# Thresholded attention and a maxout FFN on one core: another written order, other PSUM slots and other masks

## The chip, the core and the metric

The kernel runs on one core of one Trainium2 chip. The metric is the device time of one execution in microseconds (us). The core's engines run side by side, each through its own queue in program order, and wait for one another on semaphores: PE (TensorE, matrix products into PSUM; PEld is its loading of weights), DVE (VectorE), ACT (ScalarE), POOL (GpSimd) and SP (SyncE, which here only starts DMA transfers).

## The reference

```python
q, k, v: (8 batches, 8 heads, 576, 64), f32;   tau = 0.02
scores = matmul(q, k^T) / 8
keep   = scores >= max(scores, axis=-1) - tau        # else -1e9
attn   = exp(scores - max);  attn /= (sum(attn) + 1e-9)
x      = matmul(attn, v)                             # as 4608 tokens x 512
h      = maximum(maximum(x @ w1, x @ w2), x @ w3)    # 512 -> 768
out    = h @ w_out                                   # 768 -> 512
```

## The kernel before

The eight heads of a batch are taken as two quads of four heads, so there are 16 quads. Of each quad, q and k are loaded in f32, transposed on PE, copied out of PSUM, and multiplied. A *chunk* is 128 rows of queries for two of the heads; a quad has nine chunks (one of them holds the last 64 rows of all four heads), and each chunk has two *scores* of 128x576, so there are 144 chunks and 288 scores. A chunk's result P (bf16, normalized) goes through a DMA transpose from SBUF to SBUF, and with the transposed P of all nine chunks of a quad the product with v can be made (two products for each quad). The four products of a batch are the FFN's input x. The FFN of a batch is 18 hidden pieces (6 column blocks times w1, w2, w3) and two to four output pieces. The last batch's FFN is split in two parts (`SPLIT`), so that its first rows can start before the last chunks are through.

PSUM is used as four slots of 128x1024 f32. Every piece of PE work names the slot that it writes, and cannot start before the slot's former content has been read out.

The order of all this is not computed. It is a string, `ORDER`, that is read from left to right: each letter issues one step, on the engine that the step belongs to, and `_Ordered` chains the instructions of every engine in that order. Nearly all instructions pass through its helper, which is why the profile puts them all on L93. The order is thus binding within each engine (and within SP's queue of DMA starts), and free between engines. The letters, with the digit of the PSUM slot behind those of PE:

- PE: `S` one score (4 matmuls, 8 for a chunk of ninths), `T` a transposition of q or k, `O` a product with v, `F` the first half of an FFN piece and `B` its second half, `N` the out piece of a batch's last rows.
- DVE: `m` the pass over the score that gives the row maximum (z<-sc), `s` the small step from the maximum to the threshold (th), `k` the masked numerator (SCALAR_TENSOR_TENSOR with a sum), `r` the reciprocal, `c` k's way out of PSUM, `v` two thirds of the maxout, `w` a product's way out, `f` the last rows' way out.
- ACT: `e` the first pass over z, `n` the exponential with a sum, `a` q's way out of PSUM, `h` a third of the maxout, `x` a product's way out, `u` and `j` the FFN's output.
- POOL: `p` one of a chunk's two normalizing passes (P), `q` the swap of q's halves (qs; two early ones are on DVE), `y` and `z` casts of v and of the weights.
- SP: `l` loads of q, k and v, `g` loads of weights, `t` a chunk's transpose by DMA, `o` and `i` stores.

For each score one digit of `MASKED` chooses among four ways, which give the same numbers:

- 0: `m`, `s` on DVE; then two passes on ACT, `e` (a Prelu over z in SBUF, after which only the kept values count) and `n` (exponential with sum).
- 1 (masked): `m` on DVE; `e` on ACT is the exponential itself; `k` on DVE masks and sums. One pass less on ACT, one more on DVE.
- 2 and 3 (direct): as 0 and 1, but `e` reads the score from PSUM and not z, and 2 needs no `s`.

```python
def masked(g, idx, r):
    return by_mask[2 * number[g, idx] + r] in "13"
def direct(c, r):
    return by_mask[2 * number[c["g"], c["idx"]] + r] in "23"
...
def exponents(c, r):
    z = c["z", r]
    src, sign = (c[r], -1.0) if direct(c, r) else (z, 1.0)
```

So the PSUM slot of a score is free again after `m` (ways 0 and 1) or only after `e` (ways 2 and 3).

Buffers: z has 9 buffers, and 2 more in the weights' staging from the 73rd score on; P has 6; the quad's loads have 2 each; the transposed P has 2.

Of the kernel before, what the change touches and what calls it, by code (L numbers as in the profile page):

```python
# [21 lines left out]
FLAT = 2.0 ** -100  # L22

MASKED = """
232222322322222222021032222202332122123122200200111000000000100000000011
000010111020011000101000000001100001001000010011111100000000100100000000
110010030111000100010000000001010100001110001011010100110000000000000000
100101101011000000120000001010000000110011100000001110001000010011111021
"""


# [6 lines left out]
SPLIT = {7: ((0, 1), (2, 3, 4))}  # L38

ORDER = """  # L40
llllllglllT0laclT1laclzllqqS0qqS1meS2mS3lmlT0enlkS1ylmlT2eamelrnpS3leqlmnyS1qcapS0emtnrcS3pmnT2qmepgrelS1qya
gS0pmelT2mqnS3tcpemqS2nlkT1eytaS0rmnT1kpermS3yS2enczrmS1qT0enmepnqtS3nprmaymgpeS0lptS2mppT0mtpS1enencnqsS3re
rmtpS0mS1penmS3lqnsS2mtperpekzllmT0tmpenkT1pgS3eearnS0petmnqrS2meqlnpS3lmnplsS2cetpremS1pS0nmplermtzeS3mnS2p
mtnpmS3rkpS1leektS0emnrpmemptS1eekS2pO3mktS0rennmpermT2pnS1wptemS3prkyO0tmeakS2pgS1enxlnrmS0lpesS2mezT3mS1np
mgntspcS2eqrseT3mtpeS0srmapS1mnT2ptS3mnqO0ceqmeO1prswnptnkS3pxS0meF1meS2zBresmT0qghF3klpF2nkBtaS1sveS0pemF3B
nyrrsmyBepT1svS0hpcT2nS3zmaS1erpgsF2mntpsBmnS3yvF1etssT0myeBprS2cnpS3mnS0ympelF2epF3lmBnzslssvS0htBrqmeS2vpn
S1gF0sepmF3teqBmF2erssvpBtnBkphF0eS1vtS3znmF2nrBmqteS1rpvBnS3pmlnF0pmgeS1qsBsrhmS3pevS2npS1mF0npsO3ermpesmO2
zewepgsskBxtT3nF1vS2nklBarS0mlphS3mtepF2sS1rmnyBmetF3pvT0eBpcnS2tzT1nvS0asmzS3temS2qeS1meF0trkpmS3lenpBmnlys
reklpF1umerpskS3upBeoketmS0uS2umpS3tesmS1qeT0myO2nqlrsnlprcO3etqsmepwS0xptS1mnF3psnmS2BlerskpS1thF0meF3pmeBF
2ktnBveBsrS1nvpS0hmyF3emF2npBrssT0eprtvBaF1kS3nqvBeF0myhyS2kyleF3mBelBvnpS2snsS0vptemS1pnF3rmpT2tnBmpeF0scS1  # L50
htBrnmpF3erT2rpvlBasS1pstvnS2pmeF0pS3emtBqnmT2S1hcqS3empF2eS0rsqmtS1epsmBeF3pmnF0stsvBeBknF2klhF1BvelS0nrvpB
emT3pS2arvS0ptnS3mpnO1smtesrkpeF2swnlrpmeT0S1qtescS3epBmnpmnT0trskS3paS1umS0ulqmeS3lmyS1nopS2smelS0rmeS3psmn
O1ypersmqO2etkpemO0lewqxlknpS3tS1keF2momS3lexF0ktT1enkBercpnsBpumN1ertkphkF3jS0rursS1empBnmF2ptS0vpS1smeF3yt
BsnsmBpnvS0pT1hmF2atT3srepS0cF1eprBsmeqF3vnByBynvplS2nsS0plmhS1mteS2mF0nF3mteS1rrspBnmS2pelvBlepF1smT0leqBvl
aS2rkhF3oqnsS0mtS1epmBeqsF2ssmtS0epvBeyF1mnF3vpBesrS0ktphBermS1npT2svO0nytmpncT3eS1wF2nrmS0aBrsmnqF3vnT1pS0c
eBptsF2mhpS1eS3pmteS0qmBeO1spmnkteF3rvnpT0BsskapS2xvS0erS1qmtnS3pmnF2mqlespmeS1rtkBepresmT3puS1cuS0ptmnS3pS2
meyS1lrekpF0tnsmempO3lekteskO2nrsmpeBkpxrnwS1uptS3muS2pnmF0yoeS1mF3lesymBtnS2srkpS1hmBeF0spveF2ertBmpT3nrsvS
1paBlmpnS0tS3qhmF1epsmS2leBymF3tevF0nBknlS1rsvpS2esmqnBF3srmhpS1epS0tmeF2pssBrempBtesvS0ynF1mT3lnpBvF0lhsrcS
2tnT1mBnF3valS2nrBsqmeF0pvS1epS2meBptsmS3eqF1hmT2peBcS3tnskT2O0arkplnmO2lerpvewptS3xkpS1nF2meF0sstreBsmpS3nv
pBnmS1tS2hmT3eF0rmpnF1cBpnBrevptT3S2apvS0qmtS3S1enmqF2esrsqmiepmleS0soykeS1plBnmemtS3ukS0uT1snrlO2cpekynO1me  # L60
ymeF3pwxskteS0keS1BrrnkopmF2pmS0BqeuurtsmF1phS3srnpS2meT0ptBmeS3ykpaN2esvempF0tS1jkpF3ermBeS2ptvnS1pmBnS0rls
hsmpS2elF3mqntS1mpF0nsrBskpeF2lsmBetBpveF1yhvS3lnkS2lesF0mytnBmBerqsS3veF2lpvnF1pBsmT0htBceF3rT2vnpBsaS0pvnF
1qmtS2nBsrnmT0pS3hrcpF2esS1mpteS0rmpS3emBpntF1svqnS0ssBmpeoT2vO3lamtneF1wS0nrlBpmeS3qsrS2hsmS0pnmF1eptS3smeB
pmF2ntS0veS3rsmnpS1BnpO0veytrempS2empS3xsmS1tekF0nsknlT2rmpBelmlpnscS3quS1umyS2eorT0kpeO3tmeyO1ewlepsmF3etka
rknS2qklT0nBmxespcS2eryF0mpF1uskpuBtnS2BhmqF3nsvS0peS2srmtpF1eBmpeF0srvnBptS2hyS3pmeF1lmeBlBevtF3nkT2S0arrvp
BnS2mphS1smpF0ntS3smnpBmeF1lsT2esvlF3nrBrcptBnvpS2eS0qmlhS1tsnprsmT3F2epmS0aptBemF3yevS1oS0nqmBnpsrS2mnF1ptv
S0epmBeS3mthS2skeF0F1snmlBeklO3ersvpnrmByepF0swT2eqtBvnqF3ssrcS1hpiBmpT0S2vaptS1snmS0pnT3mqF2tecT1BarmS3pnS1
vqeS0mF2pesrmnptmS3npT1seS0qctBeymqermpS1eS3mpuF0nmtuskS1eS2klnS3smBesrsepO1upmemO2txrkpukeO3wnkpS0xS2emF3et
rmS1pnBssspmF2hS0rtepS3mnBpmF1etS0veF3mnN2rnpBpjF0evtF2esBkBkhF1nsvS3eBmBevO3hrkS2pwnS1mnF3prmS2eptsF0mnBpsS
1sevyS2terBmpeF3svS1iyepBmoS0yhmtF2ekF3nBsmS1ersBvpnF0pmeF2BvteS1hBmF3rsS0vpeF1rknpBBmnO2vhptO0xrpnS3pwS2trm  # L70
npS0mnF3pmteF1pBeBvtS0rS2vpS3empF1ktkF0kBereskpemBkperumO2uptO3xpN1wtenkO2jrF3pxF1hpF2nvF3tvF1rhF2pvF3pvF1hF
2tvF3vF1hF2voF3vF1ohF2vF3vF1hF2vO3vO1wF2xuuF1oF0hiF3vF1vF0hF3vF1vF0hF3vF1vF0hF3vF1vF0hF3vF1vF0huF3vF1ovF3uoF
0uoN1fjdi
"""


# [753 lines left out]
```

## Time and profile before

| | us |
|---|---|
| median of three runs | 446.71 |
| lowest and highest of them | 445.96 and 448.13 |
| span of the profiled execution, first to last instruction | 444.8 |
| PE busy in that span | 422.4 |
| ACT busy | 403.0 |
| DVE busy | 392.8 |
| POOL busy | 311.9 |

The profile gives no device time of its own for the profiled execution beside the span; the median of the runs lies 1.9 us above the span, for what stands around it and for the spread of the runs.

The page shows for every engine the busy tenths in 40 equal slices, the chain of work that ended last, groups of like instructions with the mean duration of one, and the DMA starts. A group's row has busy time, mean ns of one, and the idle time before its instructions with what ended it. Instructions on ACT and DVE overlap their neighbours a little, so what one instruction adds is the distance from its start to the next start, which is read from the timeline. The ends of matmuls are modelled, so that PE can look busy while it waits for a short time.

### The profile page before, as it was taken

The numbers are of one execution on the slowest core, as the hardware profiler recorded it, in microseconds if no ns is written. First come the engines' busy times: TensorE is split into PE (matmuls) and PEld (weight loads), VectorE is DVE, ScalarE is ACT, GpSimd is POOL, SyncE is SP. The second block draws the span as 40 slices with busy tenths as digits, with TensorE's granted clock in tenths as the row PEclk, the third lists the DMA queues.
The fourth block names the chain that finished last, engine by engine and source line by source line (L and its number), as shares of the span: only waits on it lengthen the run. The fifth ranks groups of instructions, "written<-read, shape, count | busy, mean of one in ns | idle before, by whom it ended". The sixth has DMA issues, their size and how long they took to land.

```text
span 444.8 us, 14254 instructions
## 1 busy us (share of the span) xinstructions
PE 422.4 (95%) x5188; PEld 320.2 (72%) x5190; DVE 392.8 (88%) x1228; ACT 403.0 (91%) x836; POOL 311.9 (70%) x420
## 2 busy tenths in 40 slices
PE   7767789999999999999999999999999999999996
PEld 6334347787788767787788777788688886787873
DVE  3887999999999999999999999998999998899642
ACT  3999999999999999999999999899999999987632
POOL 2799989997878687696785877676676685457400
PEclk8998999999999999999999999999999999999999
DMA  7999999999999999699899999989999977487633
GB/s 188 275 293 199 291 169 269 235 243 262 229 180 194 212 222 292 125 256 167 143 234 189 230 198 203 209 168 210 208 206 194 244 151 105 83 179 136 145 116 108
DMA packets 213959, 88.50 MB, mean 199 GB/s; under 512 B 189184, under 2 KB 202240, under 8 KB 213888
## 3 DMA queue, kind: packets, MB, share of 16 engines
q1 hardware_dynamic: 213360, 86.96, 95.9%
q8 instruction: 41, 0.67, 0.6%
q10 hardware_dynamic: 528, 0.62, 0.5%
q14 instruction: 30, 0.25, 0.2%
HBM read 35.65 MB, written 9.44 MB: 101 GB/s over the span
## 4 chain that ended last, share of the span: by engine, by line
PE 86%; ACT 5%; DVE 4%; issue 2%; DMA 1%; SPq 0%; DVEq 0%; ACTq 0%
PE ph L93 32%; PE sc L93 32%; PE po L93 10%; PE o L93 9%; ACT z L93 5%; PE tp L93 3%; DVE z L93 3%; DMA qm<-in_q_dram 1%; ACT qt L93 1%; SPq L93 0%; DVE xt L93 0%; DVE hm L93 0%; DVE stage L93 0%; DVE rs L93 0%; ACT ob L93 0%
## 5 line engine op out<-in xcount | busy, mean ns | idle before, releaser
L93 POOL TENSOR_SCALAR P<-z,rs 128x576 bf16<-128x576 f32 x250 | 200.6, 814 | 63.3 <-DVE rs L93 28.1
L93 DVE TENSOR_SCALAR_CACHE_REDUCE z<-sc 128x576 f32<-128x576 f32 x250 | 183.7, 750 | 14.8 <-PE sc L93 10.1
L93 PE MATMUL sc<-kt,qs 64*128 64x256 f32 (+2 forms) x640 | 182.6, 423 | 5.7 <-DVE z L93 2.3
L93 PE MATMUL sc<-kt,qt 64*128 64x320 f32 (+2 forms) x640 | 182.4, 433 | 5.2 <-ACT z L93 3.3
L93 PE MATMUL ph<-xt,w 64*128 64x288 bf16 (+2 forms) x2160 | 170.8, 283 | 0.1
L93 PEld LDWEIGHTS <-w 64*128 64x128 bf16 (+1 forms) x2160 | 130.1, 94 | 28.6 <-issue 4.3
L93 ACT ACTIVATE z<-z 128x576 f32<-128x576 f32 x174 | 117.6, 679 | 0.1
L93 PEld LDWEIGHTS sc<-kt,qs 64*128 64x128 f32 (+1 forms) x640 | 92.4, 180 | 25.7 <-DVE z L93 5.7
L93 ACT ACTIVATE z<-z,th 128x576 f32<-128x576 f32 x143 | 106.2, 769 | 5.0 <-DVE th L93 4.2
L93 PEld LDWEIGHTS sc<-kt,qt 64*128 64x128 f32 (+1 forms) x640 | 91.9, 179 | 19.7 <-ACT z L93 5.9
L93 DVE SCALAR_TENSOR_TENSOR z<-z 128x576 f32<-128x576 f32 x76 | 62.2, 830 | 0.5 <-ACT z L93 0.5
L93 PE MATMUL po<-wo,hT 64*128 64x512 bf16 (+3 forms) x454 | 53.5, 354 | 0.3
L93 POOL COPY qs<-qt 64x640 f32<-64x640 f32 (+3 forms) x66 | 43.0, 652 | 10.8 <-ACT qt L93 7.2
L93 ACT ACTIVATE z<-z,nm 128x576 f32<-128x576 f32 x68 | 50.6, 767 | 0.0
L93 DVE TENSOR_TENSOR hm<-ph,hm 128x576 bf16<-128x576 f32 (+2 forms) x54 | 37.0, 686 | 9.2 <-PE ph L93 8.9
L93 ACT ACTIVATE hm<-ph 128x576 bf16<-128x576 f32 (+2 forms) x54 | 31.8, 589 | 13.4 <-PE ph L93 12.8
L93 POOL TENSOR_SCALAR P<-stage,rs 128x576 bf16<-128x576 f32 x38 | 30.4, 804 | 19.3 <-ACT z L93 5.4
L93 PEld LDWEIGHTS <-hT 64*128 64x128 bf16 (+2 forms) x456 | 30.0, 95 | 16.5 <-issue 2.3
L93 DVE TENSOR_TENSOR hT<-ph,hm 128x576 bf16<-128x576 f32 (+2 forms) x54 | 37.0, 686 | 4.0 <-PE ph L93 2.3
L93 PE MATMUL o<-ptq,vb 128*64 128x64 bf16 (+2 forms) x544 | 39.0, 281 | 0.0
L93 ACT ACTIVATION_READ_ACCUMULATOR z<-z 128x1 f32 x174 | 34.3, 197 | 0.0
L93 PEld LDWEIGHTS <-vb 128*64 128x64 bf16 x544 | 23.3, 111 | 12.8 <-issue 4.9
(45 smaller groups left out, 431.6 us busy)
## 6 DMA issues: line engine op xcount, KB each, us to landing
vm<-in_v_dram SPq DMA_DIRECT2D x32, 256.0 KB, 4.8
qm<-in_q_dram SPq DMA_DIRECT2D x15, 512.0 KB, 5.0
km<-in_k_dram SPq DMA_DIRECT2D x15, 512.0 KB, 5.3
out_dram<-ob SPq DMA_DIRECT2D x14, 512.0 KB, 4.0
stage<-in_moe_w_dram SPq DMA_DIRECT2D x9, 512.0 KB, 5.2
ptq<-P SPq DMA_TRANSPOSE x144, 4.0
vr<-in_v_dram SPq DMA_DIRECT2D x16, 128.0 KB, 3.4
stage<-in_moe_w_out_dram SPq DMA_DIRECT2D x3, 512.0 KB, 4.9
```

The costliest lines, as they stand in the source:

```text
L93: ins = fn(*a, **kw)
```

## The change

`MASKED` and `ORDER` are replaced; nothing else is touched. All steps are the same and as many as before, except for those that `MASKED` decides. Of the 288 scores, before has 169 of way 0, 78 of way 1, 33 of way 2 and 8 of way 3; after has 196, 79, 9 and 4. `n` is issued 205 times (before 202), `k` 83 times (86), `s` 196 times (169). The diff, with the middle of the order cut:

```diff
 MASKED = """
-232222322322222222021032222202332122123122200200111000000000100000000011
-000010111020011000101000000001100001001000010011111100000000100100000000
-110010030111000100010000000001010100001110001011010100110000000000000000
-100101101011000000120000001010000000110011100000001110001000010011111021
+000010010201000320020000303000012100021021212010010000000010000010000110
+000011100110010011001000000000111000001001011101001010000000010000001001
+010011100010010000100001000001010000001000131011000100000000100000001000
+100010011101100100001000000110000001001120000010110100000010011000000111
 """
...
 ORDER = """
-llllllglllT0laclT1laclzllqqS0qqS1meS2mS3lmlT0enlkS1ylmlT2eamelrnpS3leqlmnyS1qcapS0emtnrcS3pmnT2qmepgrelS1qya
-gS0pmelT2mqnS3tcpemqS2nlkT1eytaS0rmnT1kpermS3yS2enczrmS1qT0enmepnqtS3nprmaymgpeS0lptS2mppT0mtpS1enencnqsS3re
-rmtpS0mS1penmS3lqnsS2mtperpekzllmT0tmpenkT1pgS3eearnS0petmnqrS2meqlnpS3lmnplsS2cetpremS1pS0nmplermtzeS3mnS2p
-mtnpmS3rkpS1leektS0emnrpmemptS1eekS2pO3mktS0rennmpermT2pnS1wptemS3prkyO0tmeakS2pgS1enxlnrmS0lpesS2mezT3mS1np
-mgntspcS2eqrseT3mtpeS0srmapS1mnT2ptS3mnqO0ceqmeO1prswnptnkS3pxS0meF1meS2zBresmT0qghF3klpF2nkBtaS1sveS0pemF3B
...
-npS0mnF3pmteF1pBeBvtS0rS2vpS3empF1ktkF0kBereskpemBkperumO2uptO3xpN1wtenkO2jrF3pxF1hpF2nvF3tvF1rhF2pvF3pvF1hF
-2tvF3vF1hF2voF3vF1ohF2vF3vF1hF2vO3vO1wF2xuuF1oF0hiF3vF1vF0hF3vF1vF0hF3vF1vF0hF3vF1vF0hF3vF1vF0huF3vF1ovF3uoF
-0uoN1fjdi
+lllllllllT3gaqqlcT2aS3lcqqgmS1lS2smeS3lsmS1nlzmeS2mnS3smgT0eslmelcaS3serqlT2qnklS0anmqqeclrpsmS1nlpS3ermlS0z
+esmepskS3gnpS2mnlpremeymS1nsspT0nypT2etzecalrpmeS0qsnT3ynmqtT1aS2lecqknpS3metpmeS0lqrskepS2mtT3prgsmeyS1ntep
+S0mlapT2smnS1rnpmS0teT3rpsmS1npsmS0eytpmnrqesscS0eymqetpeS1zntS2nmplarkS1pnlmngpssrS2ermpetS0mqelqS3nmpnsskS
+1epT2tmeO0lpremlpekS1nzS3tmnclnO1prsempeS2swzxT3tmS0epS1srakpntT3rmS2epmetyceS1pmnS3mynS0pstmnqerkS3permteS1
+pmeS2pmnS3pmetrknpS2lemS0lnpsmS1lerO3mpekqtnO0srgmnyslewpT2xkpS3arS1metF0pnmS2gpBemT3qhT1cS2npssF0rmepS3kaBq
...
+hS0srF1vepF3knpBtmBO2vhO0rxpnS1wtpsS2emF3nmS0F1semBtBrsnspvS2epS0vnS3mF1emetrmF0pnkpeBrekpkBuurtpO2uoN3puO1p
+jxO0twoF2xF1hF0vF3ivF1hF0vF3tvF2hF1vF0vF2hF1vF0vF2hF3vF0vF1hF2vO3vO1wF0xF3uF1hF0voF3vF1hF0vF2vF3hF0vF1vF3hF0
+vF2vF1hF3vF0vF1hF2vF0vF1uF2ouN1ofjdi
 """
```

More of the change, by code (lines that the diff above doesn't have):

```diff
@@ L46 @@
[L46 to L70, printed above, removed]
@@ new lines @@
+1epT2tmeO0lpremlpekS1nzS3tmnclnO1prsempeS2swzxT3tmS0epS1srakpntT3rmS2epmetyceS1pmnS3mynS0pstmnqerkS3permteS1
+pmeS2pmnS3pmetrknpS2lemS0lnpsmS1lerO3mpekqtnO0srgmnyslewpT2xkpS3arS1metF0pnmS2gpBemT3qhT1cS2npssF0rmepS3kaBq
+F2emF1ntprvBnBysvS0esS3spmhF2tzemS1lesBpmS3nzrvT0ntS1scepgT2rmaF0plnsmS2peF3smqBeT1qstvnBgS2cnpS0rmhypS1emF3
+yempF2teBkqF0lnvBnlzrBsveS3spsS1htmF2eplmS0ezBrmF3npF1svnS0perBsmpS2ntvBpngS0mhqF3meF2rtBkepS1lsnvS0pnmBS3ye
+smS1termO0plnvzgnsO3mepwteF2rkpxT0kS1aBrmeS3pshS0ssmeS1ptmF2nplS3meT0qmBetyF1rcnyT3lpBvaS0pnsvS3tznmS2eS1sym
@@ new lines @@
+teF0rmlnpkepS3BrtesmeqmT1tukF2pulcnlkS3peS0lmeS1qBrmetpmnpS3rssukS0uqS1emO2epsrmtnymO3poekpS0wxtS1npsmF3lemS
+2yBerskpS0hF1rmetF3pmeBlpS2snvlF0pemBBetvF1nlkF2hlS3rkpnBlmF0eBpsveBtvnT3F1osakS2hBlrqsmeS3yrF0nmS2nqvtS3esm
+pBeF1srpvnS2pmBetpS0mnF3spmT2hBtpceF0lnvT1BlarssS2vnqS1meqS0F3meptS2mnpBmT1thS0rscpF2emS3petS1mnBrF0sempF3ev
+ptBekF1BnvS2hsrsBtpmnF3psveT0BkaO2esvntkT1nS0rwpS3ermF2permpnS0cpnS3mytBepsmeprkT1tuS0qasS3muS1pemtS0nlmqS3e
+lmS2pS1nosmqS0elmqO3ekesrO2rpmxkpeO1twemnyS2psxF3myetrkepS1lnS0smBeykpesmS2utF1ymupT0nBrclpN2ekphktS0nF3jlmS
@@ new lines @@
+1nlsBsmeS0lrveS2plF1sempT3lBsamF0nvT3tBercpS1hkS2iqnF3smonF0mBpeF1rsrepsvBBeyrtvS2hlF3pnmS0pesS1mpnS2mtBnpmS
+0epF1rvtnpS2smBnpF3smetT0vBlaS2khlS1ermS0peF3mpF2nssmBtqeF1vnS0sBsrnmpBtevS3phS0rmqF2esqT1meBcpO0nlvpeS3ewtF
+1nrsmS2eT0kBamF3etqT0vBnycS2phtS1rsnmpS0lemS3pF2nmpO1ersmtpnkyBxsF0kteT3vBapS1revyS2nmS3yermS0pteT1mpF2nsmqe
+rsS3cqeS0mtyBepslnpmlS1epS3lmeF0pnssmqtekO1luknO3kuerwpS2eokpBxmntrrkpS3ulS1smuS2epmF0tnS3prmBnlyssmS1hoS2sm
+peF3rF0epsmBtnpsS1lvnpBmS2epF3esvT1teBmS0arkF2hqmS1teBmpnS3tspF0nmF1lnrvBpeS3vpeS2tmF0elmBnBrskphS3tseF2srvy
@@ new lines @@
+S1empF0nmBpnBrvqS1htS3pemF0pnmT2T1ncBF3aslsvS2eqrS1smepF0tmeBpBsnvpS1hsrS2pmnF3tmT0yeBpsceT1tqO2velkaO0lknle
+wS3xrpS1nmtS0ynsrS2mF3eprmF1epBmnBpssvS0eptF2smhpS3nBsmytT1nqF0veqT3cBtaS2evqS1nrsymS3peS0mlpeF2meqmeS3srBkp
+ntmelprS0elS3mpeS1mpeO0mntskO3ewnkT1nyF0celrkuS1pluBsxmnpktS3eF1surmS2puBmpeF3tkhS0S2eormpS1nlsmBpeN0mntknF1
+rvpT2jtBsapS3veF0rsmS2peBsmeqtS1sS3hlpmF2nrF0mpeBsspnS1vtS3nrmF2pnBmpeBtsvS3hrS1epmF0nptmS2nlBsqsrF3evpF1emB
+pnBvteT2F0srcphF3ntkyBS2esvpF1emBynT0vS2aBrnmlpT0S3hscqF2ertmpS0nsS1pmBemqS3eS0vptnF1smT2eBssemO3taknvF0nS2r
@@ new lines @@
+swpBemS1phS3rmepF2meS0pS1emtqBnmF3nS0svtBnrsmS1peS2rspmlO0nvpempS1xktS3qemT2eF0mntsrcnpS3leS1yrsmBlempnskS2p
+nO3meyrtpukO1epuwS2xytT0epmS3oeS1mF2alsrkeqleT3BocpelkpF0umS3uBrspemF1hF2koqBnlkBnvS0npF3rtsvS1epmBepmS2hF0r
+smpeF1BkpnT2svS3atBysmeS0veS2qtF3rempS1nmBtqF0smeS2yprsBhstmF1nylvpT3eF2kpnBtcBnS0vhS3semS1ntmF2erT0mpS3asBr
+spemS1qevS0S3npmF2ntmpF1eBmS0nsrvBpemS3tpF2ersmpS0hBknqF1ketO3vnpsmnT2BrecpF0svnF2pBtreprssS1whpBmeT3tpS0vaS
+1mnqF2tmeT3pS0cnT1BsamS3evS1tesS0rmplnF2kpemT3ieBcqnmqeS3rktpF0esmnpusS1knS3qBmeursmpteS1pS2umoS3nrmO1ussemO
@@ L74 @@
+2nynpS0xwtS3pesrmO2epmnyprS0xtS3pmeF2pmnS1BtesrmF0pohkS3peF1mS2etBsknF3smeBBtkeN2vhnkF0rjsrpvF3eBpeO2vpnS1wp
+eBmtF0nrsvpS2eS1pimnBnsF3mS2thrsrpS1emS0petmBnF2ympS1evF0pntBssmeBrvS3phS1keptF2mnF0BmnBesvF3etS1rvpF2ekBpBm
+hS0srF1vepF3knpBtmBO2vhO0rxpnS1wtpsS2emF3nmS0F1semBtBrsnspvS2epS0vnS3mF1emetrmF0pnkpeBrekpkBuurtpO2uoN3puO1p
+jxO0twoF2xF1hF0vF3ivF1hF0vF3tvF2hF1vF0vF2hF1vF0vF2hF3vF0vF1hF2vO3vO1wF0xF3uF1hF0voF3vF1hF0vF2vF3hF0vF1vF3hF0
+vF2vF1hF3vF0vF1hF2vF0vF1uF2ouN1ofjdi
 """
```

## The prediction

> **What bounds the kernel now.** I read the page first (busy shares, slices, chain), then busy time in three stretches, then the groups by shape, and last the timeline of single engines.
>
> ```profile
> span 444.8 us, 14254 instructions
> PE 422.4 (95%) x5188; PEld 320.2 (72%) x5190; DVE 392.8 (88%) x1228; ACT 403.0 (91%) x836; POOL 311.9 (70%) x420
> PE   7767789999999999999999999999999999999996
> DVE  3887999999999999999999999998999998899642
> ACT  3999999999999999999999999899999999987632
> PE 86%; ACT 5%; DVE 4%; issue 2%; DMA 1%; SPq 0%; DVEq 0%; ACTq 0%
> ```
>
> The chain lies on PE for 86%, but its first seven slices are 0.6 to 0.9 busy, and behind the first slice ACT is at nine there. The stretches show how close the others are:
>
> ```profile
> core 0: us, PE busy (x) PEld busy (x) DVE busy (x) ACT busy (x) POOL busy (x), PEclk, DMA share, GB/s
> 8.00:72.00 64.00, 50.07 (x440) 28.29 (x436) 55.76 (x169) 60.94 (x133) 55.30 (x74) 0.92 1.12 247
> 72.00:400.00 328.00, 326.74 (x4278) 257.15 (x4276) 310.51 (x987) 318.84 (x655) 242.36 (x325) 1.00 1.01 200
> 400.00:444.80 44.80, 40.38 (x426) 29.97 (x422) 25.15 (x67) 21.20 (x48) 13.52 (x17) 1.00 0.50 125
> ```
>
> Start (no FFN work exists yet): ACT is busy 60.94 of 64 us and sets the pace; PE has gaps. Middle: PE 326.74 of 328, ACT 318.84 (97%), DVE 310.51 (95%). PE's share flatters it, as the ends of matmuls are modelled; ACT and PE are level here. End: PE alone.
>
> So a term counts by stretch: ACT's work in the start in full, ACT's work in the middle in part, nothing but PE's work at the end.
>
> **Prices.** What one pass adds is its distance to the next start:
>
> ```profile
> 10.80 0.74 ACT L93 ACTIVATE z<-sc,nm 128x576 f32<-128x576 f32 x1 [0.39 <-DVE z L93]
> 11.44 0.67 ACT L93 ACTIVATE z<-z 128x576 f32<-128x576 f32 x1
> ...
> 99.98 1.44 ACT L93 ACTIVATE z<-z,th 128x576 f32<-128x576 f32 x2
> 101.31 1.44 ACT L93 ACTIVATE z<-z,nm 128x576 f32<-128x576 f32 x2
> ...
> 102.64 0.64 ACT L93 ACTIVATE xt<-o 128x576 bf16<-128x576 f32 x1
> 103.18 0.68 ACT L93 ACTIVATE z<-z 128x576 f32<-128x576 f32 x1
> ...
> 103.84 0.68 ACT L93 ACTIVATE z<-z 128x576 f32<-128x576 f32 x1
> ...
> 104.51 0.70 ACT L93 ACTIVATE qt<-tp 128x640 f32<-128x640 f32 x1
> 105.09 0.65 ACT L93 ACTIVATE hm<-ph 128x576 bf16<-128x576 f32 x1
> 105.62 0.78 ACT L93 ACTIVATE z<-z,th 128x576 f32<-128x576 f32 x1
> ```
>
> `e` from SBUF: (101.31 - 99.98) / 2 = 0.665 us; `e` from PSUM: 11.44 - 10.80 = 0.64; `n`: 103.84 - 103.18 = 0.66; `x`: 103.18 - 102.64 = 0.54; `a`: 105.09 - 104.51 = 0.58; `h`: 105.62 - 105.09 = 0.53.
>
> ```profile
> 100.91 0.15 DVE L93 TENSOR_SCALAR th<-nm 128x1 f32<-128x1 f32 x1
> 100.97 0.75 DVE L93 TENSOR_SCALAR_CACHE_REDUCE z<-sc 128x576 f32<-128x576 f32 x1
> ...
> 104.03 0.74 DVE L93 SCALAR_TENSOR_TENSOR z<-z 128x576 f32<-128x576 f32 x1
> ...
> 104.71 0.15 DVE L93 RECIPROCAL rs<-sm 128x2 f32<-128x2 f32 x1
> ```
>
> `s`: 0.06; `k`: 104.71 - 104.03 = 0.68.
>
> **The change, part by part.** I counted the letters of both strings up to the 54th score (where before's FFN begins), the 270th, the 288th, and the end.
>
> *Masks.* Of the 28 direct passes that go, 26 lie in the first 54 scores (37 there before, 11 after). Each becomes an `e` from SBUF: 26 x 0.025 = +0.65 us of ACT in the stretch that ACT sets. It also brings `s`: 21 more in that stretch, 21 x 0.06 = +1.3 us of DVE, which has 64 - 55.76 = 8.2 us free; 0, and were DVE full, 1.3. Three masked scores become unmasked: 3 x 0.66 = +2.0 us of ACT, 3 x 0.68 = -2.0 us of DVE in the whole run. Two of the three lie in the last 18 scores, where PE is the bound, and one in the first 54; the counts of letters below contain them.
>
> *Order, up to the 54th score.* After has issued one `e` more, one `n` less (0), and has F, B and `h` of the first FFN piece and one T ahead of that score: work brought forward, given back in the middle. 0 for both engines, bounds 0 and +0.5.
>
> *Order, 55th to 270th.* The same 216 S, 24 O, 64 masked scores; but 153 `n` against 149, and 214 `e` against 215: 3 x 0.665 = +2.0 us of ACT before the 270th score. Most of these are not new passes but stand further ahead in the string; behind the last score one `n` and two `e` fewer are left. If ACT sets the middle, that is 2.0 us later at the 270th score; if PE does, 0. PE's own work there is smaller by the pieces brought forward, which cancels the start.
>
> *Last 18 scores and the end.* PE's work is the same in both (16 F, 17 B, 18 S, 3 O, 1 N; then 42 F, 2 B, 5 O, 2 N).
>
> ```profile
> 407.04 5.39 PE L93 MATMUL po<-wo,hT 64*128 64x512 bf16 x48
> ...
> 422.74 0.38 PE L93 MATMUL ph<-xt,w 128*128 128x256 bf16 x2
> 423.05 0.63 PE L93 MATMUL o<-ptq,vb 128*64 128x256 bf16 x8
> ...
> 409.93 0.78 ACT L93 ACTIVATE z<-z,th 128x576 f32<-128x576 f32 x1 [2.71 <-DVE th L93]
> ```
>
> While PE works off the batch's 48 output matmuls, ACT waits 2.71 us; the two `e` and one `n` more (2.0 us) that after does ahead of the last score fit in there. The last pair of products has 18 F between its last P and itself (11 before), so its transpose is earlier. It wasn't late before (the product at 423.05 follows the hidden piece of 422.74 without a gap), so 0.
>
> *Sum for ACT:* 0.65 + 2.0 = 2.65 us up to the 270th score. Bounds 0 and +2.65. ACT is idle 9.2 of 328 us in the middle and PE 1.3, so I take the start in full and half of the middle: +0.65 + 1.0 = +1.65.
>
> *First loads.* After puts q and k of the second half ahead of the first weights, and three more scores ahead of the transposition that needs them.
>
> ```profile
> 8.00:16.00 8.00, 6.53 (x48) 3.83 (x44) 5.99 (x18) 6.29 (x16) 4.07 (x7) 0.82 1.11 262
> ```
>
> ACT is idle 1.71 of these 8 us, most of it before its first `e`, which hangs on the same first loads as before. The 0.39 us before its second `e` (first row of the prices) go: after's first `n` stands between its first two `e`s and fills them. -0.4; bounds 0 and -1.7.
>
> *The third product.* It needs the transposed P of the 18th chunk. Between the 36th `p` and the third `O` stand 9 scores, 7 `e`, 6 `n`, 2 `a` and 1 `x` before; 5 scores, 4 `e`, 3 `n` after. That is 6 x 0.665 + 2 x 0.58 + 0.54 = 5.7 us of ACT less. The timeline (start, duration, engine) has the P of that chunk as the last of four, its transpose, the product, and the first hidden piece:
>
> ```profile
> 57.57 2.90 POOL L93 TENSOR_SCALAR P<-z,rs 128x576 bf16<-128x576 f32 x4 [2.30 <-DVE rs L93]
> ...
> 65.42 1.50 SPq L93 DMA_TRANSPOSE ptq<-P  x1
> 66.99 0.66 SPq L93 DMA_DIRECT2D stage<-in_moe_w_dram  x1
> ...
> 69.39 1.18 PE L93 MATMUL o<-ptq,vb 128*64 128x512 bf16 x16
> ...
> 73.06 0.67 PE L93 MATMUL ph<-xt,w 64*128 64x288 bf16 x8
> ...
> ptq<-P SPq DMA_TRANSPOSE x144, 4.0
> ```
>
> P was there at 60.5; SP came to its transpose only at 65.42, and with 4.0 us to landing (the last row, of the page's DMA starts) the data came at about 69.4, when the product began. So 8.9 us passed, 4.9 of them in SP's queue. After has 8.9 - 5.7 = 3.2 us of room and needs 4.0 with an empty queue: 0.8 late. With the old queue it is 5.7 late. In after the three loads of the fifth quad that stood ahead of the 11th, 12th and 14th transpose stand behind the 18th, and one load of weights more ahead of it: two starts and 0.25 MB less in SP's queue. Bounds 0 (ACT's other work covers it) and +5.7; I take +0.6, near the empty queue, since the loads that filled it are moved. Behind the late product wait, on PE, the scores that follow, and then ACT.
>
> *Other transposes and loads.* After issues loads earlier (72 before the 66th transpose, 68 before) and `t` further behind its `p`. SP's wait on a full buffer then stands ahead of fewer transposes that are urgent. Bounds -0.5 and +1; 0, covered by products that begin well after their transposes.
>
> Sum: 1.65 - 0.4 + 0.6 = +1.85 us on the span: 446.65. The median lies 1.9 above the span: 448.5, that is +0.4%. One pass of DVE took 2.6 us in this execution, where its like take 0.7; if that is chance, it may be missing from the next profile and isn't counted:
>
> ```profile
> 277.13 2.60 DVE L93 SCALAR_TENSOR_TENSOR z<-z 128x576 f32<-128x576 f32 x1
> ```
>
> **A rule weighed.** The row is the middle one of the stretches: PE 326.74, ACT 318.84 of 328. The Trainium skill ("Perfetto Trace Analysis", Identifying the Most-Contended Engine) says that matmul busy time is no measure, that other engines go by occupancy, and that the fullest one bounds. By that rule ACT alone sets the middle, and the time would be that of rival 1 below. The trace doesn't settle it: ACT's 97% is the fullest of the others, yet it still leaves 9.2 us idle.
>
> **Rivals.**
>
> 1. *ACT passes everything on.* All 2.65 us, and the third product's 0.6, nothing won at the first loads: 446.7 + 3.25 = 449.95. For it: 97% occupancy. Against: PE's gaps in the middle are smaller still.
>
> 2. *Faster: slots come free earlier.* With ways 2 and 3 the slot waits for ACT. The waits from 8 to 72 us (total, times, longest):
>
> ```profile
> PEld sc L93 <- ACT z L93: 10.0, 19, 1.0
> PEld tp L93 <- ACT z L93: 4.7, 4, 2.5
> ```
>
> In the start PE's loads wait 10.0 + 4.7 us for ACT; way 0 frees the slot one pass earlier. But time is won only where ACT then idles less: at most its 3.06 us. 446.7 - 3.1 = 443.6, if ACT's idle time in 8 to 72 us falls below 1 and the middle adds nothing. Against: ACT is already nearly full.
>
> 3. *A transpose lands late.* The third product 5.7 us late with the old queue; ACT has some passes in hand and loses about 4.5 of it: 446.7 + 1.65 - 0.4 + 4.5 = 452.4. It decides from the point where SP begins that transpose over 3 us after its P. For it: in before the data came just as the product began. Against: SP's shorter queue.
>
> 4. *Nothing comes of it:* the same passes in another sequence, 446.7.
>
> **How the numbers follow.** A measurement of this kernel tells about 0.5% (2.2 us) from no change. Forecast 448.5, own range 447 to 449.8: 0.36. Rival 1, 449.95: 0.17. Rival 2, 443.6: 0.2. Rival 3, 452.4: 0.17. Rival 4, 446.7: 0.1. Faster (below 444.5): rival 2 but for a sixth, and a little of rival 4: 0.18. Slower (above 448.9): rivals 1 and 3 and a quarter of the forecast: 0.43. Same: the rest, 0.39. The range reaches from rival 2 to rival 3: 443.6 to 452.4.
>
> **What would show it.** Direct passes (z<-sc) on ACT 13 instead of 41, `th` 196. ACT busy about 405.5, PE 422. The third product near 68 to 69 us and no gap of PE ahead of it. PEld waiting for ACT in the start well below 10 us, without ACT's share there rising above 61.5 of 64. ACT 320 in the middle, over about 329 us. I am wrong if the start is shorter by more than 1 us, if PE waits for ptq, or if DVE's share in the middle rises above 96%.

## The result, and the profile after

The changed kernel takes 449.11 us (median of 6 runs, 448.48 to 450.88), the kernel before 446.50 us beside it (6 runs, 445.68 to 448.44). The ratio is 1.0065, with a 95% interval from 1.0045 to 1.0085: 2.9 us slower, give or take 0.9. The forecast was 448.5 (range 443.6 to 452.4). The time came out near it, but for the most part through other causes than the forecast had summed, as the experiments show.

The page of the changed kernel, the lines that answer to those of before:

```profile
span 448.0 us, 14336 instructions
PE 421.7 (94%) x5188; PEld 314.0 (70%) x5190; DVE 398.1 (89%) x1249; ACT 407.0 (91%) x842; POOL 316.0 (71%) x420
...
PE   8666779999999999999999999999999999999996
...
PE 74%; DVE 13%; ACT 7%; issue 4%; POOL 1%; DVEq 0%; ACTq 0%; POOLq 0%
```

The span is 3.2 us longer. PE's busy time is as it was. ACT has 4.0 us more and DVE 5.3 us more. On the chain, DVE's share went from 4% to 13%; ACT's only from 5% to 7%. Two of the three stretches (start and middle; busy time of each engine, granted clock, DMA):

```profile
core 0: us, PE busy (x) PEld busy (x) DVE busy (x) ACT busy (x) POOL busy (x), PEclk, DMA share, GB/s
8.00:72.00 64.00, 46.44 (x427) 27.81 (x425) 55.68 (x186) 60.34 (x129) 54.95 (x73) 0.97 1.12 246
72.00:400.00 328.00, 325.18 (x4240) 248.72 (x4239) 314.08 (x990) 321.24 (x664) 247.27 (x328) 1.00 1.03 204
```

In the middle DVE is now busy for 314.08 of 328 us (95.8%, before 310.51) and ACT for 321.24 (before 318.84). In the start ACT is not fuller than before. What PE waits for there did change (total, times, longest, from 8 to 72 us; first of the changed kernel, then what the kernel before waits there for DVE):

```profile
PEld sc L93 <- DVE z L93: 12.7, 15, 1.5
...
PEld sc L93 <- ACT z L93: 6.3, 6, 1.7
...
ACT z L93 <- DVE th L93: 3.2, 3, 1.8
...
PEld tp L93 <- ACT z L93: 2.0, 1, 2.0
```

```profile
PEld sc L93 <- DVE z L93: 5.9, 7, 1.8
```

The waits for ACT fell from 10.0 and 4.7 us to 6.3 and 2.0, as slots came free earlier. A wait for DVE took their place (12.7 us, before 5.9), and ACT itself now waits 3.2 us for `th`, which is the result of `s`. The groups that the change touches, first of the kernel after, then of the kernel before (instructions, busy us, mean ns of one, idle time ahead of them):

```profile
L93 DVE SCALAR_TENSOR_TENSOR z<-z 128x576 f32<-128x576 f32 x72 | 62.7, 878 | 1.4 <-ACT z L93 1.3
...
L93 DVE TENSOR_SCALAR th<-nm 128x1 f32<-128x1 f32 x196 | 26.2, 144 | 0.9
...
L93 DVE SCALAR_TENSOR_TENSOR stage<-stage 128x576 f32<-128x576 f32 x11 | 10.8, 982 | 0.0
...
L93 ACT ACTIVATE z<-sc,nm 128x576 f32<-128x576 f32 x13 | 9.4, 733 | 0.0
```

```profile
L93 DVE SCALAR_TENSOR_TENSOR z<-z 128x576 f32<-128x576 f32 x76 | 62.2, 830 | 0.5 <-ACT z L93 0.5
...
L93 DVE SCALAR_TENSOR_TENSOR stage<-stage 128x576 f32<-128x576 f32 x10 | 8.3, 826 | 0.0
```

The `k` passes became three fewer and yet took 3.0 us more (73.5 against 70.5). Their mean rose from about 830 to 878 and 982 ns, with the same work in each. That was in no term of the forecast, and the timeline shows what it is. Around 124 us of the changed kernel, DVE, then POOL, ACT and PE:

```profile
123.25 0.74 DVE L93 TENSOR_SCALAR_CACHE_REDUCE z<-sc 128x576 f32<-128x576 f32 x1
...
123.92 2.21 DVE L93 SCALAR_TENSOR_TENSOR stage<-stage 128x576 f32<-128x576 f32 x1
...
126.07 0.75 DVE L93 CAST xt<-o 128x576 bf16<-128x576 f32 x1
126.74 0.14 DVE L93 TENSOR_SCALAR th<-nm 128x1 f32<-128x1 f32 x1
...
123.35 1.46 POOL L93 TENSOR_SCALAR P<-z,rs 128x576 bf16<-128x576 f32 x2
124.79 0.74 POOL L93 TENSOR_SCALAR P<-stage,rs 128x576 bf16<-128x576 f32 x1
...
126.97 0.78 ACT L93 ACTIVATE z<-z,th 128x576 f32<-128x576 f32 x1 [0.58 <-DVE th L93]
...
126.87 0.42 PE L93 MATMUL ph<-xt,w 64*128 64x288 bf16 x4 [1.08 <-DVE th L93]
```

The `k` of the 83rd score stands from 123.92 to 126.13. Three of POOL's normalizing passes run back to back from 123.35 to 125.53. The `k` ends 0.6 us behind the last of them, which is most of what one takes undisturbed (0.74). So it had waited for all three. Behind it, the `th` came late and ACT waited 0.58 us. PE waited 1.08 us; its row names `th`, but the piece reads `xt`, whose copy, also behind the `k`, ends at 126.82.

The 2.60 us pass in the profile of before, which the prediction left out as possible chance, is the same thing:

```profile
276.94 1.46 POOL L93 TENSOR_SCALAR P<-z,rs 128x576 bf16<-128x576 f32 x2
278.38 0.74 POOL L93 TENSOR_SCALAR P<-stage,rs 128x576 bf16<-128x576 f32 x1
...
279.90 0.78 ACT L93 ACTIVATE z<-z,th 128x576 f32<-128x576 f32 x1 [1.29 <-DVE th L93]
```

The P passes end at 279.12, the `k` at 279.73. It belongs to the 194th score, and it came back at that score in every run that has this part of before's order (2.07 to 2.78 us in seven of them: x1_masks, x1_no_s, ab54, ab126, act12 and dve12 of the next section and before itself). It comes from the written order.

Where the time went is seen by matching the same piece in two traces. The table has its start in a run less its start in before, in us; the 10th and 28th F are pieces of FFN work, the last F the 180th. (Runs of the same order differ by up to 1 us in their first scores, so that only the changes along a row count. Part of that may be the granted clock: from 8 to 16 us it was 0.79 to 0.83 in before, act12 and before_k1, and 0.96 to 1.00 in the other rows.) The runs named in it are those of the next section.

| run | 8th score | 54th score | 10th F | 28th F | 198th score | 216th score | 288th score | last F |
|---|---|---|---|---|---|---|---|---|
| after | -1.6 | +2.1 | -0.5 | +2.2 | +3.3 | +1.5 | +3.1 | +3.5 |
| x1_masks | -0.7 | +2.0 | +2.2 | +2.1 | +2.1 | +2.2 | +2.2 | +2.6 |
| x1_no_s | -1.0 | -0.4 | -0.3 | -0.3 | -0.3 | -0.3 | -0.3 | -0.3 |
| act12 | +0.1 | +0.1 | +0.1 | +1.3 | +4.2 | +4.4 | +5.8 | +5.8 |
| dve12 | -0.5 | -0.5 | -0.2 | +0.4 | +4.0 | +4.9 | +6.7 | +7.0 |
| before_k1 | +0.1 | -1.5 | -1.6 | -0.3 | -0.5 | -1.8 | -2.3 | -2.3 |
| after_k1 | -2.6 | +1.0 | -1.7 | -0.6 | -0.7 | -2.4 | -2.5 | -2.1 |
| after_2k | -2.6 | +1.6 | -1.2 | +0.4 | +1.2 | -0.6 | +0.4 | +0.8 |
| b_194 | -0.1 | +0.3 | +0.3 | +0.3 | +0.3 | -1.1 | -1.1 | -0.9 |

After gains 1.6 us with its first scores (1.6 to 2.6 in the five traces that start with its order) and has lost them by the 54th, where it has also brought FFN work and a transposition forward. Level for the FFN at the 10th F (-0.5), it loses 2.7 us up to the 28th, between 90 and 136 us. The single stretched `k` above lies in that part.

### The profile page after: what moved, and what is told of

Same layout as the page of the kernel before. It is cut to its first block, busy times and chain, and to the rows that moved or that the text cites. A ratio compares the mean times of both kernels' runs of the same rounds, so it can differ in the third digit from the quotient of the medians.

```text
span 448.0 us, 14336 instructions
## 1 busy us (share of the span) xinstructions
PE 421.7 (94%) x5188; PEld 314.0 (70%) x5190; DVE 398.1 (89%) x1249; ACT 407.0 (91%) x842; POOL 316.0 (71%) x420
## 4 chain that ended last, share of the span: by engine, by line
PE 74%; DVE 13%; ACT 7%; issue 4%; POOL 1%; DVEq 0%; ACTq 0%; POOLq 0%
PE ph L93 28%; PE sc L93 26%; PE po L93 9%; DVE z L93 8%; PE o L93 7%; ACT z L93 6%; PE tp L93 3%; DVE kt L93 1%; PE warm L93 1%; DVE stage L93 1%; DVE xt L93 1%; ACT stage L93 1%; DVE th L93 1%; ACT qt L93 1%; POOL qs L93 1%
## 5 line engine op out<-in xcount | busy, mean ns | idle before, releaser
L93 PE MATMUL sc<-kt,qs 64*128 64x256 f32 (+2 forms) x640 | 180.7, 417 | 6.1 <-DVE z L93 3.2
L93 PEld LDWEIGHTS <-w 64*128 64x128 bf16 (+1 forms) x2160 | 126.2, 94 | 34.3 <-issue 5.7
L93 ACT ACTIVATE z<-z,th 128x576 f32<-128x576 f32 x169 | 127.3, 774 | 5.3 <-DVE th L93 5.0
L93 ACT ACTIVATE z<-z 128x576 f32<-128x576 f32 x178 | 120.5, 682 | 0.3
L93 POOL COPY qs<-qt 64x640 f32<-64x640 f32 (+3 forms) x66 | 47.1, 714 | 24.6 <-ACT qt L93 21.2
L93 PEld LDWEIGHTS <-hT 64*128 64x128 bf16 (+2 forms) x456 | 28.5, 95 | 17.1 <-issue 1.5
L93 PE MATMUL o<-ptq,vb 128*64 128x512 bf16 (+2 forms) x544 | 38.6, 282 | 0.3 <-DVE z L93 0.3
L93 ACT ACTIVATION_READ_ACCUMULATOR z<-z 128x1 f32 x178 | 35.6, 200 | 0.0
L93 PEld LDWEIGHTS <-vb 128*64 128x64 bf16 x544 | 22.0, 111 | 15.3 <-issue 6.1
```

The costliest lines, as they stand in the source:

```text
L93: ins = fn(*a, **kw)
```

## The experiments

Three theories were to be told apart: (A) the prediction's, ACT's extra work (masks, numerators further ahead). (B) slots freed earlier or later by the masks. (C) DVE's time: added `s`, and `k` passes held up beside POOL's P.

**One part of the change alone: masks.** Before's order, without direct passes (each `s` that becomes necessary stands right behind its `m`).

```diff
 MASKED = """
-232222322322222222021032222202332122123122200200111000000000100000000011
+010000100100000000001010000000110100101100000000111000000000100000000011
...
-llllllglllT0laclT1laclzllqqS0qqS1meS2mS3lmlT0enlkS1ylml...
+llllllglllT0laclT1laclzllqqS0qqS1mseS2mS3lmslT0enlkS1ylmsl...
```

> Before's order and slots; all 41 direct passes read z in SBUF instead of the score in PSUM (ways 2 and 3 become 0 and 1), and 33 more `s` follow their `m`. The prediction's mask term: 41 x 0.025 = +1.0 us of ACT, `s` on DVE covered: 447.5. Slots freed one pass earlier (its rival 2): 443.6, with ACT idle less than 1 us from 8 to 72 us. Nothing: 446.5. If the changed kernel's waits for DVE in the start (PEld and PE waiting for DVE's z, 19.6 us there) come from the masks, they grow here too.

Measured: 450.09 us against 446.98; ratio 1.0089 (1.0059 to 1.0119), that is +4.0 us (2.6 to 5.3; 3.1 by the medians), where the mask term had +1.0. The profiled execution was the fastest of the six, and its trace holds 2.6 us of loss. In the table 2.0 of them lie ahead of the 54th score, 0.2 between there and the 288th, and 0.4 behind it. From 8 to 72 us PE and its weight loads for scores wait 17.2 us for DVE's z, 8.5 in before: the masks alone bring most of the growth that the changed kernel shows (19.6). DVE's row shows what an `s` costs (the 0.08 us reading of the result behind each pass is left out):

```profile
48.35 0.75 DVE L93 TENSOR_SCALAR_CACHE_REDUCE z<-sc 128x576 f32<-128x576 f32 x1
...
49.15 0.15 DVE L93 TENSOR_SCALAR th<-nm 128x1 f32<-128x1 f32 x1
49.25 0.76 DVE L93 TENSOR_SCALAR_CACHE_REDUCE z<-sc 128x576 f32<-128x576 f32 x1
...
49.93 0.75 DVE L93 TENSOR_SCALAR_CACHE_REDUCE z<-sc 128x576 f32<-128x576 f32 x1
```

From `m` to `m` it is 49.93 - 49.25 = 0.68 us without an `s` and 49.25 - 48.35 = 0.90 with one: 0.22, where the prediction had 0.06 from an `s` that stood apart from its own `m`.

**The same without `s`.** This run drops tau for those 33 scores: only the row's maximum is kept in them.

```diff
-        if direct(c, r) and not masked(c["g"], c["idx"], r):
+        if flat(c, r) or direct(c, r) and not masked(c["g"], c["idx"], r):
...
-        src, sign = (c[r], -1.0) if direct(c, r) else (z, 1.0)
+        src, sign = (c[r], -1.0) if direct(c, r) else (z, -1.0 if flat(c, r) else 1.0)
...
-            th = c["nm", r] if direct(c, r) else c["th", r]
+            th = c["nm", r] if direct(c, r) or flat(c, r) else c["th", r]
```

> As x1_masks (before's order, no direct passes), but the 33 scores that would need a new `s` do without: their `m` subtracts tau and their threshold is the row's maximum, so that tau is left out for these rows. What is left of the mask change is `e` reading SBUF and slots freed one pass earlier. x1_masks lost 2.1 us between the 30th and the 54th score and nothing behind. If `s` on DVE costs that (an `s` right behind its `m` puts 0.2 us between two passes of DVE, not 0.06, and ACT waits for it): 446.5 to 447.5. If reading SBUF or the other times of the slots cost it: 449 to 450, as x1_masks.

Measured: 447.17 against 446.87; ratio 1.0013 (0.9997 to 1.0030), +0.6 us. Slots and ACT's reading of z are as in x1_masks, so (B) falls as the cause of that loss: the `s` on DVE, with ACT's wait for its result, makes 3.4 of its 4.0 us (2.8 of 3.1 by the medians). (In the one profiled execution of x1_masks the granted clock was also 0.72 from 54 to 60 us, where it was 1.00 in before. So the trace alone doesn't separate the two; the times of 6 and 12 runs do.)

**Start and rest apart.** Before's steps up to a score, then after's order for what isn't done, or the reverse.

```diff
-...mnqO0ceqmeO1prswnptnkS3pxS0meF1meS2zBresmT0qghF3klpF2nk...
+...mnqO0ceqmeO1prswnptnkS3pxS0zyyF1gBemhT2F1rmepS3kaBqF0em...
```

> Before's order, slots and masks up to the 54th score, then after's for all that isn't done by then. If the loss comes from the start (masks, loads, the order of the first three chunks' worth of quads): 446.5. If it comes behind the 54th score (numerators further ahead on ACT, or DVE's `k` held up beside POOL's P): 449. The traces lie between them: after is 2.1 us behind at the 54th score but has 1.3 us of PE's work brought forward, and 3.2 behind at the end, so 448.5 here.

> The reverse: after's order, slots and masks up to the 54th score, then before's. Loss in the start: 449. Loss behind it: 446.5. By the traces (0.8 us of loss by the 54th score beside the work brought forward): 447.3.

> After's order up to the 126th score, then before's. If the loss is made between 90 and 135 us, as the offsets of hidden pieces in the two traces say (-0.5 us at the 10th, +2.2 at the 28th): 449. If numerators further ahead cost a little everywhere: 447.5 to 448. If nothing is lost up to there: 446.5.

Measured: ba54 450.21 against 446.98 (ratio 1.0078, 1.0060 to 1.0095), ab54 449.39 (1.0059, 1.0043 to 1.0076), ab126 451.75 (1.0112, 1.0093 to 1.0130). Both halves are slow, and their losses don't add up to after's 2.9 us: the seam costs something of its own (ba54 goes from +1.8 at its 60th score to +6.4 at its 66th). As a division of the loss these runs are inconclusive. They showed two other things. From the 10th to the 28th F, ba54 loses 2.7 us and ab126 2.8, as after does. And the same scores have the long `k` each time: the 83rd with 2.21 us in ba54 and 2.28 in ab126, the 224th with 2.18 in ba54 (2.17 in after).

**`k` with one input, in both kernels.** The multiplication by z is left out.

```diff
-            vector.scalar_tensor_tensor(out=z, in0=z, scalar=thr, in1=z,
-                                        op0=OP.is_ge, op1=OP.mult, accum_out=acc)
+            vector.tensor_scalar(out=z, in0=z, scalar1=thr, scalar2=None,
+                                 op0=OP.is_ge, op1=OP.add, accum_out=acc)
```

> Before, with `k` as a pass with one input from SBUF (a comparison and a sum; the multiplication by z is left out, so the masked scores' numerators are 1 or 0). Its 86 passes took 829 ns in the mean against 740 undisturbed. Held up by POOL's P passes for its second input: the long ones (2.6 us) go, DVE's `k` group falls by at least 86 x 0.09 = 7 us, and the time falls by up to 2 us to 444.5. If the long passes have another cause they stay, and so does the time, 446.5, but for what a shorter pass gives.

> After, with the same `k` as the run beside it (one input from SBUF, no multiplication by z). If after's loss is `k` held up beside P (892 ns against 829, about 5 us more in the sum), the 2.6 us between the kernels shrink to under 1: equal to the run beside it. If the loss is ACT's passes further ahead, the 2.6 us stay.

Measured: before_k1 443.40 against 446.76 (ratio 0.9926, 0.9905 to 0.9946), after_k1 444.56 (0.9953, 0.9935 to 0.9970). The distance between the two kernels shrinks from 2.9 to 1.2 us by the ratios, and to 0.1 by the profiled spans (442.4 and 442.5; before_k1's profiled execution was 0.8 us above its median, after_k1's 0.3 below). From the 10th F to the last, before_k1 gains 0.7 us on before and after_k1 0.35: of the 3.9 us that after loses there, 0.35 are left in these traces. Where the rest of the 1.2 us lies, they don't show. The groups of `k` and P in before_k1:

```profile
L93 DVE TENSOR_SCALAR_CACHE_REDUCE z<-z 128x576 f32<-128x576 f32 x76 | 55.8, 744 | 0.4 <-ACT z L93 0.3
...
L93 POOL TENSOR_SCALAR P<-z,rs 128x576 bf16<-128x576 f32 x250 | 183.3, 744 | 81.0 <-DVE rs L93 35.0 <-ACT z L93 11.7 <-DVE th L93 11.1
```

The `k` takes 0.74 us in the mean. The mean of the 288 P passes falls with it, from 813 to 744 ns: the two engines had held up one another. POOL's busy time falls by 22.4 us in before and 25.6 in after.

**The disputed cost by itself.** A program of DVE and POOL passes alone; its output is zeros.

```diff
+    stage(0, two, None)      # k alone
+    stage(1, None, norm)     # P alone
+    stage(2, two, norm)      # k beside P
+    stage(3, single, norm)   # one SBUF input beside P
+    stage(4, psum, norm)     # input from PSUM beside P
```

> Only passes of DVE and POOL in five stages of 12, the output is zeros: `k` alone; P alone; `k` beside P; a pass with one SBUF input and a sum beside P; a pass from PSUM with a minimum beside P. If two SBUF inputs collide with P: `k` about 0.74 us alone, 1.4 to 2.2 beside P, and the other two stay as they are alone (0.7). If any SBUF pass collides: both one-input stages are longer too.

Measured, from the timelines: one `k` alone, seven of POOL's P passes and two `k` beside them (third stage), two passes with one input beside P (fourth):

```profile
6.32 0.74 DVE L41 SCALAR_TENSOR_TENSOR z<-z 128x576 f32<-128x576 f32 x1
...
23.19 8.62 POOL L53 TENSOR_SCALAR P<-y,rs 128x576 bf16<-128x576 f32 x7
...
25.15 1.18 DVE L41 SCALAR_TENSOR_TENSOR z<-z 128x576 f32<-128x576 f32 x1
...
26.37 1.18 DVE L41 SCALAR_TENSOR_TENSOR z<-z 128x576 f32<-128x576 f32 x1
...
39.86 0.75 DVE L45 TENSOR_SCALAR_CACHE_REDUCE z<-z 128x576 f32<-128x576 f32 x1
...
40.65 0.75 DVE L45 TENSOR_SCALAR_CACHE_REDUCE z<-z 128x576 f32<-128x576 f32 x1
```

The groups of the stages from PSUM and with one input:

```profile
L49 DVE TENSOR_SCALAR_CACHE_REDUCE z<-sc 128x576 f32<-128x576 f32 x12 | 9.1, 756 | 0.3
L45 DVE TENSOR_SCALAR_CACHE_REDUCE z<-z 128x576 f32<-128x576 f32 x12 | 9.0, 752 | 0.3
```

The stages ran into one another at their borders, but the rows are plain: a pass with two SBUF inputs takes 1.18 us beside P and 0.75 alone; with one input or from PSUM it takes 0.75 beside P as well. Beside each other, one `k` and one P pass come every 1.22 us (26.37 - 25.15; 8.62 / 7 = 1.23).

**What a microsecond of ACT or DVE costs in the middle.** Twelve more passes in before, on either engine, at the same twelve scores.

```diff
             exponents(c, r)
+            if 54 <= x_ < 270 and x_ % 18 == 9:
+                scalar.activation(out=c["z", r], in_=c["z", r], func=AF.Copy)
...
             maximum(c, r)
+            if 54 <= x_ < 270 and x_ % 18 == 9:
+                vector.tensor_scalar(out=c["z", r], in0=c["z", r], scalar1=1.0, scalar2=None,
+                                     op0=OP.mult, op1=OP.min, accum_out=c["nm", r])
```

> Before, with 12 more ACT passes (a copy of z onto itself behind `e`, every 18th score from the 64th to the 262nd): 12 x 0.665 = 8.0 us of ACT. The prediction let half of ACT's extra work in the middle through: +4.0, 450.5. ACT as the bound there: up to +8.0 less the 9.2 us that ACT is idle only in part, 453 to 454.5. PE as the bound: 446.5 to 447.5.

> Before, with 12 more DVE passes of one SBUF input (z onto itself behind `m`, the same scores as the 12 of ACT): 12 x 0.7 = 8.4 us of DVE, spread. ACT's 12 gave +5.4. If DVE's load as such sets the middle: +5 to +8, 452 to 455. If DVE has room (310.5 of 328 us busy) and only single long passes hurt: +1 to +2.5, 447.5 to 449.

Measured: act12 452.19 against 446.76 (ratio 1.0125, 1.0106 to 1.0145), +5.6 us for 8.0 us of work. dve12 453.88 against 446.87 (1.0155, 1.0136 to 1.0174), +6.9 us for about 8.4. So 0.7 of an added microsecond of ACT goes through, and 0.8 of one of DVE (each give or take 0.1, by the intervals). That DVE has room was wrong. The middle of dve12, its stretch from 72 to 400 us:

```profile
72.00:400.00 328.00, 323.65 (x4175) 249.91 (x4173) 312.95 (x992) 313.37 (x642) 239.34 (x320) 1.00 0.98 195
```

DVE's share rises only from 310.51 to 312.95 us although it has 8.4 us more to do; the whole pipeline stretches instead, with ACT and PE both less busy than before.

**Two instructions of after alone.** The `k` of the 83rd and of the 224th score with one input.

```diff
-        if masked(c["g"], c["idx"], r):
+        if 2 * number[c["g"], c["idx"]] + r in (82, 223):
+            vector.tensor_scalar(out=z, in0=z, scalar1=thr, scalar2=None,
+                                 op0=OP.is_ge, op1=OP.add, accum_out=acc)
+        elif masked(c["g"], c["idx"], r):
```

> After, with the `k` of two scores alone, the 83rd and the 224th, as a pass with one input from SBUF (no multiplication by z for these two). These took 2.21 and 2.17 us, in after and again in each run that has this part of after's order. If being held up by POOL's P passes is what costs after its time: the 83rd gives 1 to 1.5 us of the 2.7 that are lost between the 10th and the 28th hidden piece, the 224th 0.5 to 1: 446.6 to 447.6. If collisions don't matter one by one, only DVE's load (2.9 us less of 398): 448.5 to 449.

Measured: 447.39 against 446.87; ratio 1.0009 (0.9993 to 1.0025). Of after's 2.9 us 0.4 are left, give or take 0.7. The place that was shown above, now:

```profile
123.38 0.74 DVE L93 TENSOR_SCALAR_CACHE_REDUCE stage<-stage 128x576 f32<-128x576 f32 x1
...
124.72 0.14 DVE L93 TENSOR_SCALAR th<-nm 128x1 f32<-128x1 f32 x1
...
125.30 1.43 ACT L93 ACTIVATE z<-z,th 128x576 f32<-128x576 f32 x2
```

Behind it `th` comes 1.34 us after the start of `k` (2.82 in after), and ACT doesn't wait. In the table after goes from -0.5 at the 10th F to +3.5 at the last, this run from -1.2 to +0.8: 2.0 us less from two instructions.

**One letter of before.** All is computed; the `k` of the 194th score stands behind the next `s`, `v` and `m`.

```diff
-...T0ptBmeS3ykpaN2esvempF0tS1jkp...
+...T0ptBmeS3ypaN2esvemkpF0tS1jkp...
```

> Before, computing all that it did, with one letter moved: the `k` of the 194th score stands behind the next `s`, `v` and `m` of DVE. It took 2.60 us there, held up by three P passes, with ACT 1.29 and PE 0.94 us idle for what stood behind it. If that is the cost: -0.9 to -1.4 us, 445.3 to 445.8. If the time is made up elsewhere anyway: 446.5.

Measured: 445.20 against 446.87; ratio 0.9958 (0.9941 to 0.9975), 1.9 us faster; 1.4 us of it at that very place (+0.3 at the 198th score, -1.1 at the 216th). It beats both kernels and computes the same. DVE there, and the last of POOL's three passes:

```profile
277.43 0.15 DVE L93 TENSOR_SCALAR th<-nm 128x1 f32<-128x1 f32 x1
...
277.52 0.76 DVE L93 TENSOR_TENSOR hm<-ph,hm 128x576 bf16<-128x576 f32 x1
278.20 0.75 DVE L93 TENSOR_SCALAR_CACHE_REDUCE z<-sc 128x576 f32<-128x576 f32 x1
...
278.87 1.15 DVE L93 SCALAR_TENSOR_TENSOR z<-z 128x576 f32<-128x576 f32 x1
...
278.68 0.74 POOL L93 TENSOR_SCALAR P<-stage,rs 128x576 bf16<-128x576 f32 x1
```

The `k` still collides, with the last of the three P passes, but takes 1.15 us, and the `th` for which ACT had waited is ahead of it.

## Why the prediction was right, and where it wasn't

- *The bound.* That ACT sets the start, and that ACT and PE are level in the middle, left DVE out. That is the step that failed. DVE was 95% busy in the middle and counted as covered, yet dve12 shows that added time on it goes through at 0.8, no less than ACT's at 0.7. The chain of before, with DVE at 4%, doesn't tell that.
- *Masks, +0.65 us of ACT, `s` covered.* Mis-sized, and on the wrong engine. Masks alone (all 41 direct scores, where after changes 28 of them) cost 4.0 us in before's order and 0.6 without the `s`. These 0.6 (-0.1 to 1.3 by the interval) neither show nor exclude ACT's share. An `s` right behind its `m` costs 0.22 us of DVE, not 0.06, and it wasn't covered. How much of this is in after's own start wasn't tried separately. By the strings, 7 of its 29 `s` ahead of the 54th score follow their own `m` on DVE with nothing between (3 of 8 in before), so an estimate from these two prices is 4 x 0.22 + 17 x 0.06 = 1.9 us of DVE, not 1.3.
- *Order up to the 54th score, 0.* At the first F after is 0.6 us earlier, at the 10th 0.5: as forecast.
- *Order from the 55th to the 270th, ACT's +1.0.* The rate was guessed low (a half; 0.7 measured), but there is little sign of the term itself: with all `k` undisturbed, after_k1 loses 0.3 us more than before_k1 from the 10th F to the last. What after loses there is, by these traces, DVE's: its `k` passes that POOL's P holds up. This cause was missing in the sum. The prediction saw one such pass and left it out as possible chance.
- *Last 18 scores and the end, 0.* The offset goes from 3.2 us at the 270th score to 3.5 at the last F: as forecast.
- *First loads, -0.4.* After is 1.6 us earlier at the 8th score (the bound was -1.7), and 0.3 later at the 18th. The gain was there and was used up. Not all of it need be the loads': x1_masks and x1_no_s, with the loads of before, are 0.7 and 1.0 us earlier at the same score.
- *Third product, +0.6.* It came at 68.26, inside the 68 to 69 forecast and 1.1 earlier than in before. SP was free when its P was ready, as assumed, but the transfer was in time. Rival 3 fell. SP's transpose and the product in after:

```profile
64.39 1.29 SPq L93 DMA_TRANSPOSE ptq<-P  x1
...
68.26 1.18 PE L93 MATMUL o<-ptq,vb 128*64 128x512 bf16 x16
```

- *What would show it.* 13 direct passes, 196 `th`, PE 421.7, ACT's 60.34 in the start: right. ACT 407.0 where 405.5 was said, and 321.24 in the middle where 320 was. DVE's 95.8% in the middle lies just under the 96% that was named as the sign of an error.
- *Rivals.* Rival 2 had the mechanism (slots free earlier; PE's waits for ACT fell by 6.4 us) and lacked what is late next: DVE. Rival 1 named a time close to the result (449.95) for ACT's reason, which the runs don't bear out. The rule weighed with it, that the fullest engine bounds ("Perfetto Trace Analysis" in the Trainium skill, Identifying the Most-Contended Engine), would have left DVE out as well: ACT is the fullest, and DVE's time costs no less.

That the total was near is luck: the product's +0.6 was not there and the runs show little of ACT's +1.65, while `s` and the held `k` on DVE, which the sum had at nothing, cost as much.

## What to carry to other kernels

When three engines are over 94% busy, as in the middle here, and pass work around in a ring, none of them is cover for another: price added time on each at most of its length, or measure that rate with a dozen idle passes as here. A pass that takes three times its like isn't chance until the other engines' rows at that moment have been read; here it came back at the same score in each run of the same order, and moving one letter won 0.4%. And price a short dependent instruction where it will stand: right behind its producer it cost 0.22 us, elsewhere 0.06.

## What the runs showed of the hardware

- A DVE pass with two SBUF inputs and POOL's pass that reads SBUF hold each other up: 0.75 us alone, 1.18 side by side, while a DVE pass with one SBUF input or with its input in PSUM (both with a sum or a minimum) stays at 0.75. As one of each comes every 1.22 us, about 0.6 us of a pass seem to exclude the other engine, not the whole 0.75; that is an estimate from these rows. It fits the `k` in the kernels, which ended 0.6 us behind the last P pass.
- The Trainium skill says this on the page "SBUF — State Buffer", section "Who interferes with whom": such a DVE instruction contends with a GpSimd instruction that reads SBUF, and the contention is an exclusive lock. The rows agree (1.18 us beside P, 0.75 with one SBUF input).
- In the stage program the two alternate (1.18 us for each `k`). In the kernel a `k` waited for three P passes in a row (2.21 and 2.60 us). Why POOL isn't made to give way there is open.
- The hold goes both ways: with one-input `k`, POOL's P passes fell from 813 to 744 ns in the mean.
